# One head's queries and keys on the even partitions, the other's on the odd ones

## The chip, the cores and the metric

The kernel runs on one core of a Trainium2 chip. The metric is the device time of one execution in microseconds (us). Three executions of the kernel before took 274.06, 274.38 and 275.83 us; the median is 274.38. The profile is of another execution.

## The reference

Two stages. First, attention within chunks of 64 positions: 8 batches, 8 heads, 576 positions (9 chunks) and 64 features a head.

```
scores = q_c @ k_c^T / sqrt(64)          # per batch, head and chunk: 64x64
attn   = softmax(scores)                 # with 1e-9 added to the sum
out    = attn @ v_c                      # 64x64
```

The heads of a position are put side by side, which gives x of 4608 tokens by 512. Then a mixture of 8 experts: a token goes to the expert with the largest logit of x @ w_gate; each expert keeps the 80 tokens (the capacity) with the largest gate weight, and its rows of the output are gate * (relu(x @ w1[e]) @ w2[e]) (512 to 1024 to 512 features). All other rows of the output are zero. Everything is float32.

## The kernel before, in words

**Tiling of attention.** The positions are regrouped into 36 tiles of 128 rows (two chunks), taken two at a time in 18 pairs n = 0 to 17. One tile has four pairs of heads; the two heads of a pair lie on the 128 partitions, 64 features each.

**The buffers of queries and keys.** There are six (`qbufs`, L320), each 128 partitions by three blocks of 512 columns. On the lower 64 partitions (head 0) block 0 holds keys and block 1 queries; on the upper 64 (head 1) block 1 holds queries and block 2 keys. The rest, block 0 above and block 2 below, is set to zero once (L649, L650) and stays zero. So one matmul with block 1 as stationary operand and blocks 0 and 2 as moving operand (L344) gives the scores of both heads side by side: the contraction runs over all 128 partitions, and the zeros keep the heads apart. `load_qk` (L323) fills a buffer with two DMAs, one for each head: 64 rows of 4 KB (keys and queries side by side), 256 KB each. In DRAM the rows of a head lie next to each other.

**The buffers of values.** Six (`vbufs`, L330), filled by `load_v` (L333) with two DMAs of 64 rows of 2080 bytes each: head 0's rows go to the even partitions and head 1's to the odd ones, each to columns of its own. The score difference is written in the same interleaved order (L358), so the transposed probabilities match.

**One pair n in the loop (L697).** TensorE's order is written out by hand: `scores(n)` (L337), the transpose of x for the gate of pair n-3, `values` of pair n-2 (L380), the transpose of the probabilities of pair n-1 (L373), and on some pairs matmuls of the gate and of a threshold count. VectorE takes the row maxima and subtracts them (`maxima`, `minus`), divides by the sums (`divide`, L409), and does steps of the gate. ScalarE does the exponentials and the copies out of PSUM. SyncE issues the DMAs in program order: in iteration n the qk loads of pair n+3, the value loads of pair n+1 and, for tiles that are not kept on chip, a store of x to a scratch tensor `xs` in DRAM. Each buffer is overwritten three pairs later, and a load waits until its last reader is done. The framework works out these waits from the parts of buffers that instructions touch, and also makes a DMA wait for an earlier one of the same group of semaphores to land, so only some of them are under way at a time.

**Before and behind the loop.** The memsets of buffers and the first loads come first (L647 to L681): buffer 0 is set to zero by VectorE and loaded by SyncE, buffer 1 by GpSimd and ScalarE, the others by VectorE and SyncE. 25 matmuls without a use run meanwhile. From pair 15 on, SyncE also stores the tiles of x that were kept (1 MB each, L735) and loads the weights of the first two experts (`early_weights`, L631). Then comes a gating stage that finds each expert's tokens by a threshold, gathers of tokens by GpSimd from `xs` (L179), and the expert stage (L173 on), whose matmuls fill TensorE while SyncE loads weights of 2 MB and writes zero rows of the output.

Of the kernel before, what the change touches and what calls it, by code (L numbers as in the profile page):

```python
# [17 lines left out]
P = 128  # L18
# [39 lines left out]
def attention_moe(ctx: ExitStack, tc: tile.TileContext, qk, vv, wg, w1, w2, cap, cst, out):  # L58
# [225 lines left out]
    with ExitStack() as actx:  # L284
# [38 lines left out]
        def load_qk(i, eng=nc.sync):  # L323

            d = QKV["qk", i] = qbufs[i % (2 * NB)]
            for h in range(2):
                eng.dma_start(d[64 * h:64 * h + 64, 512 * h:512 * h + 1024],
                              qk[i // 2, i % 2, 64 * h:64 * h + 64])

        vbufs = [wk.tile([P, 2, VW], F32, name=f"vb{j}", tag=f"vb{j}", bufs=1)  # L330
# [313 lines left out]
        with tc.manual_schedule():  # L644
            warm = gk.tile([P, 2 * P], BF16, name="warm", tag="lv", bufs=LV)
            nc.vector.memset(warm, 0.0)
            for j, qb in enumerate(qbufs):  # L647
                eng = nc.gpsimd if j == 1 else nc.vector
                eng.memset(qb[64:P, 0:512], 0.0)  # L649
                eng.memset(qb[0:64, 1024:1536], 0.0)  # L650
                if j < 2:
                    load_qk(j, (nc.sync, nc.scalar)[j])
            nc.scalar.dma_start(ident, cst[:, C_ID:C_ID + P])
# [15 lines left out]
            for i in (2, 3):  # L669
                load_qk(i)  # L670
            for i in (0, 1):
                load_v(i)
            for i in (4, 5):
                load_qk(i)
# [407 lines left out]
```

## Time and profile before

| | |
|---|---|
| median of three runs | 274.38 us (274.06 to 275.83) |
| profiled execution | 277.03 us, of which its span 275.2 us |
| busy: TensorE matmul | 232.4 us (84%) |
| busy: VectorE / ScalarE / GpSimd | 119.0 / 66.5 / 57.0 us |
| DMA | 84.73 MB, mean 308 GB/s |
| qk loads | 70 on SyncE, 256 KB, 6.7 us from issue to landing (median); two more on ScalarE |
| value loads | 72 on SyncE, 130 KB, 6.6 us |
| weights of the experts | 12 loads of 2 MB and 8 of 1 MB |
| chain that ended last | `qb<-in_qk` 24%, first expert layer 16%, second 15% |

How to read it: the engines run beside each other, so their busy times don't add up to the span. The chain that ended last follows the last instruction back to what released it, step by step; its shares say what set the end. "Landing" is the time from a DMA's issue on a queue to its last byte. The profiled execution is 2.65 us longer than the median of the timed ones.

### The profile page before, as it was taken

The page shows a single profiled execution, that of the slowest core. Times are in us where ns is not written, and L with a number is a line of the kernel's source. Part 1 is how long each engine was busy: PE and PEld are TensorE (multiplying, and loading weights), DVE is VectorE, ACT ScalarE, POOL GpSimd, SP SyncE. Part 2 cuts the span into 40 slices and gives each one's busy share as a digit, 9 for nine tenths or more (in the row PEclk, how much of TensorE's full clock was granted, in tenths as well). Part 3 has the DMA queues.
Part 4 walks back from the last instruction along what each step waited for, and adds up shares of the span by engine and source line. Part 5 has one row for each costly group of instructions (what it writes and reads, how often), then busy time and mean ns, then how long its engine had stood idle before and what let it go on. Part 6 is the DMA issues. An engine that isn't in the chain of part 4 may idle for free.

```text
span 275.2 us, 7328 instructions
## 1 busy us (share of the span) xinstructions
PE 232.4 (84%) x3117; PEld 149.7 (54%) x3117; DVE 119.0 (43%) x263; ACT 66.5 (24%) x115; POOL 57.0 (21%) x167
## 2 busy tenths in 40 slices
PE   6773989979788977978868885899999999999990
PEld 4763778968667866766756574234333433333320
DVE  6545366876574846665735846011111211212110
ACT  1012123453251625352614410112020201101000
POOL 8003000121122222222373845300000000000081
PEclk9599799999999999999979779599999999999996
DMA  7998999999999999999999999999999999999431
GB/s 157 237 255 220 233 239 238 274 257 260 232 239 284 288 230 215 276 271 272 365 394 402 409 411 415 393 396 393 409 413 405 407 415 409 416 395 409 182 133 69
DMA packets 35718, 84.73 MB, mean 308 GB/s; under 512 B 4000, under 2 KB 4128, under 8 KB 35680
## 3 DMA queue, kind: packets, MB, share of 16 engines
q1 hardware_dynamic: 34416, 80.73, 93.0%
q0 software_dynamic: 960, 2.88, 2.7%
q10 hardware_dynamic: 304, 0.59, 1.0%
q8 instruction: 27, 0.44, 0.7%
q14 instruction: 11, 0.09, 0.1%
HBM read 64.00 MB, written 20.45 MB: 307 GB/s over the span
## 4 chain that ended last, share of the span: by engine, by line
PE 51%; DMA 39%; SPq 3%; POOL 3%; issue 2%; POOLq 0%; DVE 0%
DMA qb<-in_qk 24%; PE hc L204 16%; PE yc L237 15%; DMA vb<-in_vv 5%; PE o L403 5%; PE s L344 5%; DMA xs<-kept 4%; DMA w<-in_w 4%; DMA xgc<-xs,gic 2%; PE hpc L222 2%; SPq L335 2%; PE pt L369 2%; PE px L369 1%; PE xpc L192 1%; PE small L455 1%
## 5 line engine op out<-in xcount | busy, mean ns | idle before, releaser
L344 PE MATMUL s<-qb 128*64 128x128 f32 x576 | 42.3, 298 | 21.7 <-DMA qb<-in_qk 20.0
L344 PEld LDWEIGHTS s<-qb 128*64 128x64 f32 x576 | 35.6, 150 | 27.0 <-issue 22.4
L204 PE MATMUL hc<-w,xtc 128*32 128x512 f32 x384 | 45.6, 618 | 0.0
L237 PE MATMUL yc<-w,htc 128*32 128x512 f32 x384 | 42.3, 592 | 0.0
L403 PE MATMUL o<-vb,pT 128*64 128x130 f32 x576 | 38.0, 283 | 3.3 <-DMA vb<-in_vv 2.6
L354 DVE TENSOR_REDUCE mx<-s 128x16 f32<-128x1024 f32 x18 | 22.0, 1225 | 36.8 <-PE s L344 36.7
L403 PEld LDWEIGHTS o<-vb,pT 128*64 128x64 f32 x576 | 33.1, 139 | 4.8 <-issue 3.7
L237 PEld LDWEIGHTS yc<-w,htc 128*32 128x32 f32 x384 | 12.4, 110 | 28.3 <-issue 28.3
L204 PEld LDWEIGHTS hc<-w,xtc 128*32 128x32 f32 x384 | 12.6, 113 | 27.3 <-issue 26.7
L446 ACT COPY xT<-px 128x1024 f32<-128x1024 f32 x17 | 17.2, 1013 | 42.3 <-PE px L369 42.3
L378 ACT ACTIVATE pT<-pt 128x1024 f32<-128x1024 f32 x18 | 18.4, 1023 | 32.1 <-PE pt L369 32.1
L256 POOL DMA_INDIRECT out<-ysc,to x6 | 6.0, 993 | 88.5 <-SPq L933 86.1
L359 DVE TENSOR_TENSOR sm<-s,mx 128x1024 f32<-128x1024 f32 x18 | 22.1, 1228 | 0.6
L209 ACT ACTIVATE hsc<-hc 128x512 f32<-128x512 f32 x6 | 3.6, 597 | 65.3 <-PE hc L204 65.3
L242 DVE TENSOR_SCALAR ysc<-yc,gatec 128x512 f32<-128x512 f32 x6 | 4.5, 751 | 33.5 <-PE yc L237 33.5
L418 DVE TENSOR_TENSOR x<-o,rc 128x1024 f32<-128x1024 f32 (+1 forms) x14 | 15.0, 1072 | 0.5
L211 DVE TENSOR_SCALAR hsc<-hc 128x512 f32<-128x512 f32 x6 | 4.1, 691 | 25.2 <-PE hc L204 25.2
L520 POOL TENSOR_SCALAR u<-sx 128x4 f32<-128x4 f32 x8 | 1.6, 195 | 62.1 <-DVE sx L519 38.9
L369 PE MATMUL pt<-ct,sm 64*128 64x64 f32 x288 | 12.8, 229 | 1.2 <-ACT pT L378 1.2
L226 DVE COPY htc<-hpc 128x512 f32<-128x512 f32 x6 | 4.2, 692 | 22.0 <-PE hpc L222 22.0
L369 PEld LDWEIGHTS pt<-ct,sm 64*128 64x128 f32 x288 | 10.3, 139 | 4.3 <-issue 3.0
L545 ACT ACTIVATE lv<-io_b,bo 128x256 bf16<-128x256 bf16 x29 | 12.5, 497 | 0.4 <-DVE bo L526 0.4
(136 smaller groups left out, 233.8 us busy)
## 6 DMA issues: line engine op xcount, KB each, us to landing
w<-in_w SPq DMA_DIRECT2D x12, 2048.0 KB, 18.8
qb<-in_qk SPq DMA_DIRECT2D x70, 256.0 KB, 6.7
vb<-in_vv SPq DMA_DIRECT2D x72, 130.0 KB, 6.6
out<-zero SPq DMA_DIRECT2D x9, 1024.0 KB, 16.3
w<-in_w SPq DMA_DIRECT2D x8, 1024.0 KB, 12.6
xs<-x SPq DMA_DIRECT2D x10, 512.0 KB, 6.5
xs<-kept SPq DMA_DIRECT2D x3, 1024.0 KB, 8.8
xs<-x SPq DMA_DIRECT2D x4, 256.0 KB, 10.7
```

The source lines that it names most:

```text
L204: nc.tensor.matmul(h[o:o + 32, :], lhsT=xT[r][:, b, o:o + 32], rhs=getw(groups[r][g])[0][:, b, 512 * f:512 * f + 512], start=(b == 0), sto ...
L237: nc.tensor.matmul(y[o:o + 32, :], lhsT=hT[r][c // 4][:, c % 4, o:o + 32], rhs=getw(groups[r][g])[1][:, c, :], start=(c == 0), stop=(c == ...
L256: i = nc.gpsimd.indirect_dma_start(out=out, out_offset=bass.IndirectOffsetOnAxis(ap=to, axis=0), in_=ys, in_offset=None, bounds_check=NT * ...
L344: nc.tensor.matmul(ps[64 * u:64 * u + 64, t, P * pr:P * pr + P].rearrange("p (h k) -> p h k", h=2), lhsT=t8[:, 1, pr, u, :], rhs=t8[:, 0:3 ...
L354: nc.vector.tensor_reduce(d['mx'], d['s8'], axis=AX.X, op=ALU.max)
L359: nc.vector.tensor_tensor(d['sm'].rearrange("p c k h -> p h c k"), d['s8'], d['mx'][:, :, :, None].to_broadcast([P, 2, 8, 64]), op=ALU.sub ...
L369: nc.tensor.transpose(pm[:, u, 64 * c:64 * c + 64], src(c)[rows], ident[rows, rows])
L378: nc.scalar.activation(d['pT'], pt, AF.Exp, scale=0.125)
L403: nc.tensor.matmul(po[64 * u:64 * u + 64, o:o + 130].rearrange("p (h x) -> p h x", h=2), lhsT=d['pT'][:, u, c:c + 64], rhs=v[:, :, pr, u, ...
L418: nc.vector.tensor_tensor(TT[T][:, r:r + nt, :].rearrange("p r (k h e) -> p (r k) h e", k=4, h=2), pov[..., 0:64], rc[:, :, :, None].to_br ...
L446: nc.scalar.copy(dst, pm)
L545: nc.scalar.activation(lv, io_b, AF.Sign, bias=bo[:, rt:rt + 1], scale=-1.0)
```

## The change

`load_qk` writes head h to the partitions h, h+2, ..., that is to the even ones (h = 0) or the odd ones (h = 1). Columns, row size, source and queue are as before. As the zero parts are now every second partition of a block, the two memsets cover all 128 partitions of blocks 0 and 2, and the loads overwrite half of each. The score matmuls are the same; they sum over the partitions in another order.

```diff
             d = QKV["qk", i] = qbufs[i % (2 * NB)]
             for h in range(2):
-                eng.dma_start(d[64 * h:64 * h + 64, 512 * h:512 * h + 1024],
+                eng.dma_start(d[h:P:2, 512 * h:512 * h + 1024],
                               qk[i // 2, i % 2, 64 * h:64 * h + 64])
...
             for j, qb in enumerate(qbufs):
                 eng = nc.gpsimd if j == 1 else nc.vector
-                eng.memset(qb[64:P, 0:512], 0.0)
-                eng.memset(qb[0:64, 1024:1536], 0.0)
+                eng.memset(qb[:, 0:512], 0.0)
+                eng.memset(qb[:, 1024:1536], 0.0)
                 if j < 2:
                     load_qk(j, (nc.sync, nc.scalar)[j])
```

## Rows read from the trace of the kernel before

**Rows 1.** The page's 40 slices of the span: DMA busy tenths, and GB/s.

```profile
DMA  7998999999999999999999999999999999999431
GB/s 157 237 255 220 233 239 238 274 257 260 232 239 284 288 230 215 276 271 272 365 394 402 409 411 415 393 396 393 409 413 405 407 415 409 416 395 409 182 133 69
```

**Rows 2.** Busy time by stage: stretch, length, five engines, PEclk, DMA share, GB/s.

```profile
34.92:130.31 95.39, 81.77 (x1554) 70.42 (x1551) 61.66 (x113) 38.02 (x60) 17.19 (x76) 1.00 1.04 255
...
141.24:173.80 32.56, 25.31 (x305) 20.21 (x305) 18.19 (x84) 7.29 (x20) 17.95 (x43) 0.81 1.04 410
173.80:268.40 94.60, 94.23 (x836) 32.27 (x836) 12.59 (x20) 10.16 (x18) 7.15 (x12) 0.98 0.95 369
```

**Rows 3.** The chain in order of time: start us, us, what.

```profile
62.91 7.26 DMA qb<-in_qk
...
128.17 1.19 SPq L335
```

**Rows 4.** Waits of all engines: total us, times, longest us.

```profile
PE s L344 <- DMA qb<-in_qk: 20.0, 12, 4.7
```

**Rows 5.** Waits of SyncE's queue: total us, times, longest us.

```profile
SPq L327 <- DMA qb<-in_qk: 18.1, 31, 1.2
```

**Rows 6.** Timeline of SyncE: start us, us, line, operation, names, count.

```profile
8.47 2.41 SPq L335 DMA_DIRECT2D vb<-in_vv  x4
...
23.00 6.30 SPq L327 DMA_DIRECT2D qb<-in_qk  x10
...
126.06 3.30 SPq L335 DMA_DIRECT2D vb<-in_vv  x4
...
146.51 3.78 SPq L426 DMA_DIRECT2D xs<-x  x2
```

**Rows 7.** DMA issues near 23.0, 28.7, 126.1, 128.2, 146 to 152, 166 to 176: landing us.

```profile
qb<-in_qk SPq DMA_DIRECT2D x1, 256.0 KB, 3.5
...
qb<-in_qk SPq DMA_DIRECT2D x1, 256.0 KB, 7.9
...
vb<-in_vv SPq DMA_DIRECT2D x1, 130.0 KB, 5.8
...
vb<-in_vv SPq DMA_DIRECT2D x1, 130.0 KB, 4.6
...
xs<-x SPq DMA_DIRECT2D x4, 256.0 KB, 10.7
...
xgc<-xs,gic POOLq DMA_INDIRECT x6, 6.5
```

**Rows 8.** Timeline of TensorE, score and value matmuls: start us, us, [wait <- releaser].

```profile
34.92 1.97 PE L344 MATMUL s<-qb 128*64 128x128 f32 x32
...
42.12 1.97 PE L344 MATMUL s<-qb 128*64 128x128 f32 x32
...
59.20 1.09 PE L344 MATMUL s<-qb 128*64 128x128 f32 x16
...
131.14 1.99 PE L403 MATMUL o<-vb,pT 128*64 128x130 f32 x32
...
141.24 3.32 PE L403 MATMUL o<-vb,pT 128*64 128x130 f32 x32 [2.57 <-DMA vb<-in_vv]
```

**Rows 9.** Timeline of all engines from the start of the span.

```profile
0.73 4.06 SPq L327 DMA_DIRECT2D qb<-in_qk  x6
...
1.15 0.48 DVE L649 MEMSET qb<- 64x512 f32 x1 [0.16 <-issue]
1.29 0.52 POOL L650 MEMSET qb<- 64x512 f32 x1
...
1.78 0.48 DVE L650 MEMSET qb<- 64x512 f32 x1
...
7.52 0.93 DVE L655 MEMSET vb<- 128x1040 f32 x1 [0.17 <-issue]
...
30.07 1.70 PE L344 MATMUL s<-qb 128*64 128x128 f32 x16 [0.38 <-DMA qb<-in_qk]
```

## The prediction

> **What bounds the kernel now.** I read the slices of the page first. The DMA row stands at nine tenths or more from the second slice to the 37th (but for one at eight), yet the row of GB/s under it has two levels: 215 to 288 in slices 2 to 19, 365 to 416 in the next 18 [rows 1]. The 16 DMA engines count as busy in both; in the first they move far less. The table by stage puts numbers on it. From the fifth score block to the end of the last (34.92 to 130.31 us) the DMA share is 1.04 at 255 GB/s, while TensorE is busy 81.77 of 95.39 us; in the gating stage behind it the share is again 1.04, but at 410 GB/s; in the expert stage TensorE is busy 94.23 of 94.60 us [rows 2]. So attention is held by slow transfers and the experts by TensorE. The chain of waits says the same: it runs for long stretches through `qb<-in_qk`, in pieces such as one of 7.26 us [rows 3], and among TensorE's waits the score matmuls on that transfer lead with 20.0 us [rows 4]. SyncE too waited 18.1 us, 31 times, for an earlier qk load to land before it issued the next [rows 5]. All this is one queue that drains slowly.
>
> **How slow, and compared with what.** Ten qk loads of 256 KB are issued back to back, the first at 23.00 us, one every 0.63 us [rows 6]; the first lands 3.5 us after its issue, the tenth (issued 9 x 0.63 later, at 28.7) 7.9 us after [rows 7]. So they land (28.7 + 7.9 - 23.0 - 3.5) / 9 = **1.12 us apart**, 234 GB/s. The control is in the same kernel: a value load also moves 64 rows, but to every second partition. Four are issued from 126.06 us [rows 6]; the first lands 5.8 us after issue, the fourth, issued at 128.17 [rows 3], 4.6 after [rows 7]: (128.2 + 4.6 - 126.1 - 5.8) / 3 = 0.30 us for 130 KB, with some 0.03 of rounding, which scales to 0.53 to 0.65 us for 256 KB. The 410 GB/s of the gating stage [rows 2], where weights go to all 128 partitions, gives 256 KB / 410 = **0.64 us**. I take 0.64. What separates the qk loads from both is the 64 neighbouring partitions.
>
> [...]
>
> **The change, part by part.**
>
> *The loads.* Count, bytes and queue stay: 72 loads of 256 KB, each with 64 rows. Each goes from 1.12 to 0.64 us. Per pair that is 4 x 0.64 + 4 x 0.30 for the value loads, plus 1.3 for a 512 KB store at 410 GB/s where there is one: 5.1 us of DMA. SyncE needs 8 issues per pair, or 9 with a store, in ten of the 18 pairs: at 0.63 us each, as the ten qk loads went out [rows 6], 5.0 or 5.7, on average 5.4 us. TensorE's pace where no wait shows is (59.20 - 42.12) / 3 = 5.69 us a pair [rows 8]. So TensorE becomes the bound, with SyncE close behind.
>
> (a) *From the fifth score block to the last*, now 95.39 us. If only TensorE's idle time goes, it saves 95.39 - 81.77 = 13.6 us [rows 2]. At the pace of 5.69, 13 blocks and the last one's 1.97 take 75.9 us, and 19.5 are saved [rows 8]. The three blocks of the pace lack the threshold tallies that every second pair has from the ninth on, and busy time holds them, so I take a value nearer the first: **15.5**, ends 13.6 and 19.5.
>
> (b) *The start.* The fourth score block's second half runs at 30.07 us, after a wait for its load [rows 9]. In the code that load's second half is the 23rd issue on SyncE from the value load at 8.47 us on [rows 6]. At 0.63 us each it goes out at 8.47 + 22 x 0.63 = 22.3, and lands 3.5 - (1.12 - 0.64) = 3.0 us later, at 25.3: 4.8 us earlier, of which I take **4.5** for waits that stay. SyncE's waits for earlier landings are what goes here; the issue rate is late next. Ends: 3, if most of these waits stay, and 6, if the small loads among the 22 issue faster.
>
> (c) *The tail of attention.* The last two value blocks wait 2.57 us for `vb`, then take 3.32 us, where two others took 1.99 [rows 8]. Their loads sit in the queue behind stores and weights that SyncE issued late. With SyncE no longer behind, both go: 2.57 + 1.33 = 3.9. Ends 0 and 3.9; **3**, as the stores of the kept tiles and the first experts' weights still crowd that queue.
>
> (d) *The gather.* The first gather of tokens takes 6.5 us beside a backlog of weights [rows 7]; with the backlog gone earlier it might take the 3.5 of a load into a short queue [rows 7]. Ends 0 and 3; **1**. The expert stage itself moves as a block, covered by TensorE's 94.23 busy us. Were weights late there, TensorE would wait; it does not now, and their loads will meet a shorter queue.
>
> *The memsets.* They keep their 512 columns and double their partitions. A 64x512 one takes 0.48 us on VectorE, a 128x1040 one 0.93 [rows 9], so partitions are free: 0.
>
> *A wait added at the start.* The memsets now touch partitions that the first loads write. SyncE's first load waits for VectorE's memset of columns 0:512 (end 1.63 us in place of its issue at 0.73), the second for that of 1024:1536 (2.26 us) [rows 9]; four more qk loads are queued behind, all before the value load that is held until 8.47 us anyway. ScalarE's two loads wait for GpSimd's memsets, the second of which ends at 1.81 us [rows 9]; the load of the identity is behind them. About 0.9 us late, against four loads that drain 4 x 0.48 = 1.9 us faster: 0, already inside (b). If the loads stayed slow, up to 1 us would show.
>
> **Sum:** 15.5 + 4.5 + 3 + 1 = 24. The profiled execution took 277.03 us (span 275.2), 2.65 above the median of 274.38; none of the terms is known to be in that difference, so I take the sum off the median: 274.4 - 24 = **250.4** (and 253 for a run like the profiled one).
>
> **The rivals.**
>
> *Another engine binds first.* SyncE has 5.4 of 5.69 us filled, and its instructions wait in order for TensorE's release of buffers. If these waits add 0.9 us a pair, the pace is 6.5, the stretch 13 x 6.5 + 2 = 86.5, and (a) falls to 8.9; with (b) and nothing for (c) and (d), 274.4 - 13.4 = 261. Against it: loads run three pairs ahead, so a lag of one pair costs nothing. Chance 0.08.
>
> *Nothing changes.* [...] Chance 0.05.
>
> *Slower.* The two halves of a buffer now interleave by partitions and share columns 512:1024. If the planner that places waits treats them as one block, the second half's load waits for the first to land: 3.0 - 0.64 = 2.4 us, twice a pair. SyncE's pace becomes 5.4 + 4.8 = 10.2 us, the stretch 13 x 10.2 + 2 = 135, 39 more than now: about 313. It decides above some 0.85 us of wait per half, where 5.4 + 1.7 reaches today's (95.39 - 1.97) / 13 = 7.2 us a pair. Against it: the last stores of `x` write interleaved blocks of rows of one tensor, and the second went out within 3.78 us of the first [rows 6], though such stores take 10.7 us to land [rows 7]. Chance 0.07.
>
> *The forecast* keeps 0.80; its own range is 274.4 - 33 = 241 to 274.4 - 16.6 = 258, by the ends of the terms. All upper ends together are unlikely, so the range starts at 243; it reaches to 262 to take in the busy SyncE. About 1% (2.7 us) is what a measurement of this kernel can tell from no change. Faster by more: 0.80 + 0.08 = 0.88; same: 0.05; slower: 0.07.
>
> **What would show it.** In the profile after: `qb` loads that land about 0.64 us apart, GB/s near 300 in attention at a DMA share clearly under 1, the score matmuls' wait on `qb` down from 20 us to a few, score blocks 5.7 to 6.0 us apart, the fourth block's second half near 25.5, no 2.57 us at the last value blocks. Blocks 6.5 apart with TensorE idle would mean SyncE or VectorE; landings still 1.12 apart, that partitions are not the cause; a gap of some 3 us between the two halves' issues, the planner's wait. The forecast is wrong if the experts then wait for weights and give the gain back.

## The result, and the profile after

The change made the kernel **5.5% faster**: medians of 259.81 us after and 274.69 us before (four runs each), ratio 0.9446, 95% interval 0.9403 to 0.949. The forecast was 250.4 with a range of 243 to 262: the direction and the range held, the gain was 14.9 us where 24 had been forecast. The profiled execution after took 258.25 us (span 256.5), 1.6 below its median, while that of before lay 2.3 above its own; of the 18.7 us between the two spans some 3.9 are therefore differences between executions, not the change.

The slices of the page after, DMA busy tenths and GB/s, against [rows 1]:

```profile
DMA  5888988998998799999999999999999999999241
GB/s 197 277 254 270 366 299 281 312 337 281 299 293 290 249 289 312 329 319 347 397 406 411 412 417 389 397 393 411 418 408 402 416 408 411 410 397 404 107 162 38
```

The attention part moves about 250 to 370 GB/s in place of 215 to 288, and the DMA engines are no longer full there. The table by stage of the kernel after, in the columns of [rows 2] (attention from the fifth score block to the end of the last, the stretch from there to the first gather, the experts):

```profile
33.53:111.96 78.43, 78.43 (x1554) 69.78 (x1551) 61.40 (x113) 37.48 (x60) 16.71 (x75) 1.00 0.91 297
111.96:146.76 34.80, 28.09 (x400) 22.64 (x400) 21.15 (x75) 12.60 (x28) 18.47 (x55) 0.85 1.04 391
154.45:248.66 94.21, 94.21 (x836) 31.78 (x836) 12.30 (x19) 10.16 (x18) 6.96 (x11) 0.98 0.96 372
```

In the first stretch TensorE is busy for all of its 78.43 us: it is the bound now. A DMA share of 1.04 is reached only in the stretch behind it. What the transfers do, first SyncE's timeline after (against the ten loads of [rows 6]):

```profile
20.03 6.29 SPq L327 DMA_DIRECT2D qb<-in_qk  x10
```

and the landing times of its first, fourth, ninth and tenth load (issued near 20.0, 21.9, 25.1 and 25.7 us, as in [rows 7]):

```profile
qb<-in_qk SPq DMA_DIRECT2D x1, 256.0 KB, 3.1
...
qb<-in_qk SPq DMA_DIRECT2D x1, 256.0 KB, 4.5
...
qb<-in_qk SPq DMA_DIRECT2D x1, 256.0 KB, 4.5
...
qb<-in_qk SPq DMA_DIRECT2D x1, 256.0 KB, 5.7
```

The fourth and the ninth wait equally long, so from one to the other loads land as far apart as they are issued: (25.1 - 21.9) / 5 = 0.64 us, with some 0.02 of rounding. From the first to the tenth, as the 1.12 us of before were worked out, it is (25.7 + 5.7 - 20.0 - 3.1) / 9 = 0.92 us, because two landings in between came over a microsecond late: the third load took 4.3 us where the second took 3.1, and the tenth took 5.7. Now TensorE's timeline after, with the columns of [rows 8]:

```profile
23.89 1.09 PE L344 MATMUL s<-qb 128*64 128x128 f32 x16 [2.20 <-DMA qb<-in_qk]
...
26.48 1.98 PE L344 MATMUL s<-qb 128*64 128x128 f32 x16 [1.50 <-DMA qb<-in_qk]
...
29.43 3.51 PE L403 MATMUL o<-vb,pT 128*64 128x130 f32 x32
33.53 1.97 PE L344 MATMUL s<-qb 128*64 128x128 f32 x32
...
110.00 1.97 PE L344 MATMUL s<-qb 128*64 128x128 f32 x32
...
121.51 2.00 PE L403 MATMUL o<-vb,pT 128*64 128x130 f32 x32 [0.96 <-DMA vb<-in_vv]
```

The pace of the score blocks is (110.00 - 33.53) / 13 = 5.88 us. The waits of the kernel after (total us, times, longest), against [rows 4]:

```profile
PE s L344 <- DMA qb<-in_qk: 7.6, 5, 2.8
...
POOL w L639 <- DMA xs<-kept: 2.5, 1, 2.5
...
PE o L403 <- DMA vb<-in_vv: 1.0, 1, 1.0
```

The wait for qk loads fell from 20.0 to 7.6 us, all of it at the start. And the chain of waits after, in the tail (start us, us, what):

```profile
121.19 11.78 DMA xs<-kept
...
133.08 0.31 POOL w L639 x2
...
146.76 6.44 DMA xgc<-xs,gic
```

A store of a kept tile needs 11.78 us to land, GpSimd waits for it with a copy into a weight buffer (L639, which holds back the second expert's weights), and what GpSimd does next stands on the way to the gather.

### The profile page after: what moved, and what is told of

The parts are those of the page before. It is cut to its first block, busy times and chain, and to the rows that moved or that the text cites. A ratio compares the mean times of both kernels' runs of the same rounds, so it can differ in the third digit from the quotient of the medians.

```text
span 256.5 us, 7329 instructions
## 1 busy us (share of the span) xinstructions
PE 229.5 (89%) x3117; PEld 148.0 (58%) x3117; DVE 118.5 (46%) x263; ACT 66.1 (26%) x115; POOL 56.8 (22%) x167
## 4 chain that ended last, share of the span: by engine, by line
PE 76%; DMA 11%; DVE 3%; POOL 3%; issue 2%; SPq 1%; ACT 1%; POOLq 0%; ACTq 0%
PE hc L204 17%; PE yc L237 16%; PE o L403 13%; PE s L344 12%; DMA xs<-kept 5%; PE pt L369 4%; PE px L369 4%; DMA qb<-in_qk 4%; PE small L455 3%; DMA xgc<-xs,gic 3%; PE hpc L222 2%; PE xpc L192 1%; DVE qb L650 1%; DVE qb L649 1%; SPq L335 1%
## 5 line engine op out<-in xcount | busy, mean ns | idle before, releaser
L344 PE MATMUL s<-qb 128*64 128x128 f32 x576 | 38.2, 287 | 7.7 <-DMA qb<-in_qk 7.6
L344 PEld LDWEIGHTS s<-qb 128*64 128x64 f32 x576 | 33.4, 144 | 10.8 <-issue 6.8
L237 PEld LDWEIGHTS yc<-w,htc 128*32 128x32 f32 x384 | 12.4, 110 | 28.3 <-issue 28.3
L211 DVE TENSOR_SCALAR hsc<-hc 128x512 f32<-128x512 f32 x6 | 4.2, 692 | 25.3 <-PE hc L204 25.3
## 6 DMA issues: line engine op xcount, KB each, us to landing
w<-in_w SPq DMA_DIRECT2D x8, 1024.0 KB, 12.4
```

Source lines behind the costliest of these rows:

```text
L237: nc.tensor.matmul(y[o:o + 32, :], lhsT=hT[r][c // 4][:, c % 4, o:o + 32], rhs=getw(groups[r][g])[1][:, c, :], start=(c == 0), stop=(c == ...
L344: nc.tensor.matmul(ps[64 * u:64 * u + 64, t, P * pr:P * pr + P].rearrange("p (h k) -> p h k", h=2), lhsT=t8[:, 1, pr, u, :], rhs=t8[:, 0:3 ...
```

## The experiments

For each, the stretch of 40 to 100 us gives one row (length, five engines, PEclk, DMA share, GB/s). GB/s divided by the DMA share is an estimate of what the engines would move if they were never idle: the pace of the transfers themselves, value loads and stores included. Kernel before: 256 / 1.05 = 244.

```profile
40.00:100.00 60.00, 52.37 (x1009) 45.34 (x1007) 38.83 (x73) 23.89 (x38) 10.91 (x48) 1.00 1.05 256
```

Kernel after: 294 / 0.91 = 323.

```profile
40.00:100.00 60.00, 60.00 (x1187) 53.45 (x1183) 46.30 (x88) 28.32 (x47) 13.38 (x60) 1.00 0.91 294
```

**E1, the wide memsets alone.** The kernel before with

```diff
-                eng.memset(qb[64:P, 0:512], 0.0)
-                eng.memset(qb[0:64, 1024:1536], 0.0)
+                eng.memset(qb[:, 0:512], 0.0)
+                eng.memset(qb[:, 1024:1536], 0.0)
```

> The wide memsets alone: qk loads go to the lower and upper 64 partitions as before. Theory (the partitions that a load reaches set its pace): landings stay about 1.12 us apart, the DMA share in attention stays near 1.04 at 255 GB/s, time within 1% of before (272 to 277.5; the first loads go out 0.9 us later). Rival (the memsets' new form, after which VectorE finishes a microsecond sooner and the value loads start earlier, gives part of the gain): 270 or less.

Measured: 275.41 us, ratio 1.003 (0.997 to 1.009). Its row:

```profile
40.00:100.00 60.00, 53.28 (x1008) 46.51 (x1006) 40.28 (x75) 24.57 (x39) 10.91 (x48) 0.97 1.04 261
```

261 / 1.04 = 251, near the 244 of before. The whole gain comes with the loads' partitions, and the late first loads cost nothing that can be measured.

**E2, half of the loads.** The kernel after, but only even buffers interleaved (memsets to match):

```diff
-                eng.dma_start(d[h:P:2, 512 * h:512 * h + 1024],
+                rows = slice(h, P, 2) if i % 2 == 0 else slice(64 * h, 64 * h + 64)
+                eng.dma_start(d[rows, 512 * h:512 * h + 1024],
```

> Only buffers 0, 2 and 4 are loaded to every second partition, the odd ones to 64 neighbouring partitions. Theory (transfers no longer bind once a pair's DMA time is below TensorE's 5.88 us): a pair needs 2 x 0.64 + 2 x 1.12 + 4 x 0.30 and 1.3 for a store in ten of 18 pairs, on average 5.4 us, so the pace of the score blocks stays near 5.9 and the time is 259 to 263. Rival (each load that is made faster gives its share): half of the gain, 266 to 269.

Measured: 263.91 us, ratio 0.9615 (0.929 to 0.994). Its row, and three score blocks of its TensorE timeline:

```profile
40.00:100.00 60.00, 58.08 (x1137) 51.24 (x1131) 45.40 (x84) 28.33 (x46) 12.62 (x56) 1.00 1.00 280
```

```profile
52.33 1.97 PE L345 MATMUL s<-qb 128*64 128x128 f32 x32
...
87.64 1.09 PE L345 MATMUL s<-qb 128*64 128x128 f32 x16
...
114.27 2.18 PE L345 MATMUL s<-qb 128*64 128x128 f32 x32
```

280 / 1.00 = 280 lies half way between 244 and 323, yet the six blocks from the first of these rows to the second take (87.64 - 52.33) / 6 = 5.89 us each, as in the kernel with all loads interleaved. From 87.64 on blocks wait for loads again, and the last four take (114.27 - 87.64) / 4 = 6.66 us each. So half of the change gives the whole pace for a while, which fits loads that were issued ahead being used up, and then the transfers bind again: the theory holds only for the first part, and its 5.4 us of DMA a pair were too few. The interval of the time is too wide to tell theory and rival apart by itself.

**E3, another order of the first loads.** The kernel after with

```diff
-            for i in (2, 3):
+            for i in (2, 3, 4, 5):
                 load_qk(i)
-            for i in (0, 1):
-                load_v(i)
-            for i in (4, 5):
-                load_qk(i)
-            for i in (2, 3):
+            for i in (0, 1, 2, 3):
                 load_v(i)
...
-            for i in range(4, NBV):
-                load_v(i)
...
                     if n < 2:
                         load_qk(2 * (n + NB) + 1)
+                    if n == 0:
+                        for i in range(4, NBV):
+                            load_v(i)
```

The last two value buffers are now loaded behind the qk loads of pair 3.

> The changed kernel with its first loads in another order: the qk loads of buffers 4 and 5 ahead of the first value loads, in the time in which SyncE waited for VectorE's memset of a value buffer, and the last two value buffers behind the qk loads of pair 3. Theory (the start is held by when SyncE can issue, and the waits cost twice since the clock falls after them): the fifth score block starts at 25 to 28 us in place of 33.5, and the total is 253 to 256. Rival (SyncE's 5.4 us of issuing per pair becomes the bound as soon as TensorE starts earlier): the last score block ends at 109 us or later in place of 112, total 257 to 260.

Measured: 257.8 us, ratio 0.9394 (0.919 to 0.960). Score blocks of its TensorE timeline, the fifth and the last's second half:

```profile
28.09 1.97 PE L344 MATMUL s<-qb 128*64 128x128 f32 x32
...
107.73 1.09 PE L344 MATMUL s<-qb 128*64 128x128 f32 x16 [0.48 <-DMA qb<-in_qk]
```

its waits:

```profile
POOL w L639 <- DMA xs<-kept: 3.3, 1, 3.3
PE o L403 <- DMA vb<-in_vv: 2.7, 1, 2.7
```

and its chain:

```profile
146.45 6.49 DMA xgc<-xs,gic
```

The fifth block starts 5.4 us earlier and the last ends 3.1 us earlier (108.8 against 112.0), but the gather goes out at 146.45 against 146.76: both waits in the tail grew, and the gain is gone before the gather. The rival's total (257 to 260) came out, but neither side had this reason. By its interval the time can't be told from that of the change (0.9446).

**E4, the kept stores early, on SyncE's queue.**

```diff
-DEFER = {15: [0], 16: [2], 17: [4]}
+DEFER = {6: [0], 10: [2], 11: [4]}
```

> The changed kernel, with the three stores of the kept tiles (1 MB each) issued in pairs 6, 10 and 11, which store nothing else, in place of 15, 16 and 17. Theory (the tail behind attention is held by the DMA queue: GpSimd waits 2.5 us for the last kept store and the last value blocks wait for their loads): both waits go, and the time falls by 2 to 4.5 us to 255 to 258. Rival (the tail is held by its chain of small steps, or attention has no DMA time to spare): within 1 us of the changed kernel, or above it.

Measured: 261.82 us, ratio 0.9541 (0.938 to 0.971). Its waits and its chain:

```profile
PE s L344 <- DMA qb<-in_qk: 12.4, 8, 4.4
```

```profile
149.67 6.42 DMA xgc<-xs,gic
```

The wait of GpSimd for the store went, and its last score block ends at 117.5, so the stretch to the gather is 32.2 us in place of 34.8: the theory's half on the tail holds. But attention lost 5.5 us: the score matmuls' wait for qk loads rose from 7.6 to 12.4 us, which fits each 1 MB store standing ahead of qk loads in the one queue. The sum is as the rival had it; by its interval the time can't be told from that of the change.

**E5, 64 neighbouring partitions from 32 to 95.** The kernel after with

```diff
-            for h in range(2):
-                eng.dma_start(d[h:P:2, 512 * h:512 * h + 1024],
-                              qk[i // 2, i % 2, 64 * h:64 * h + 64])
+            src = qk[i // 2, i % 2]
+            eng.dma_start(d[32:96, 0:1024], src[0:64])
+            eng.dma_start(d[0:32, 512:1536], src[64:96])
+            nc.scalar.dma_start(d[96:P, 512:1536], src[96:P])
```

> Head 0 goes in one load to the 64 neighbouring partitions 32 to 95, head 1 in two loads of 32 rows to partitions 0 to 31 (SyncE) and 96 to 127 (ScalarE's queue); no load uses every second partition. Theory (what counts is that a load covers parts of both the lower and the upper 64 partitions): head 0's loads are as fast as interleaved ones, about 0.64 us per 256 KB, GB/s in attention near 297, time 258 to 264. Rival (what counts is that the rows of a load are not neighbours): 256 KB stay near 1.1 us, GB/s near 255, 270 to 276.

Measured: 289.07 us (four executions from 284.02 to 289.38), where the kernel before, measured beside it, took 275.56. Its row, and SyncE's waits:

```profile
40.00:100.00 60.00, 49.94 (x906) 43.51 (x902) 36.57 (x66) 21.52 (x33) 8.17 (x37) 0.94 0.73 216
```

```profile
SPq L336 <- DMA qb<-in_qk: 19.0, 13, 4.7
```

The time is far from both expectations, and for a reason that neither had: SyncE's value loads (L336) waited 19.0 us, 13 times, for qk loads to land. Its chain points to those on ScalarE's queue: a qk load goes out straight behind a score block at 58.40 us, with no issue of SyncE between, lands 3.10 us later, and a value load follows at 61.52. The transfers themselves have a pace of 216 / 0.73 = 296, well above the 244 of loads to the lower or upper half, though none of this kernel's qk loads goes to every second partition. Single loads say it more directly. Four on SyncE's queue, issued at 27.04, 28.19, 28.74 and 29.42 us, go in turn to partitions 0 to 31 (128 KB) and 32 to 95 (256 KB); their landing times:

```profile
qb<-in_qk SPq DMA_DIRECT2D x1, 128.0 KB, 5.3
...
qb<-in_qk SPq DMA_DIRECT2D x1, 256.0 KB, 4.8
...
qb<-in_qk SPq DMA_DIRECT2D x1, 128.0 KB, 5.0
...
qb<-in_qk SPq DMA_DIRECT2D x1, 256.0 KB, 5.0
```

So they land at 32.3, 33.0, 33.7 and 34.4 us. The 256 KB across the middle come some 0.65 us behind the load ahead of them, as interleaved ones do; the 128 KB in one half take as long for half the bytes. So the pace doesn't need rows that aren't neighbours: these 64 rows, with 32 in each half, have it.

**E6, opposite halves on two queues.** The kernel before, with loads of odd buffers on ScalarE's queue, upper half first:

```diff
-            for h in range(2):
+            if i >= 2 and i % 2:
+                eng = nc.scalar
+            for h in ((1, 0) if i % 2 else (0, 1)):
```

> The layout of before, but loads of odd buffers go out on ScalarE's queue, upper half first, so that transfers to the lower and to the upper 64 partitions are more often under way together. Theory (each half of the partitions takes data at a limited pace of its own): GB/s in attention rises from 255 to 275 or more and the time falls to 262 to 271. Rival (one transfer to 64 neighbouring partitions is slow whatever runs beside it): 272 or more, GB/s near 255.

Measured: 279.17 us, ratio 1.012 (1.005 to 1.019). Its row, and a wait of ScalarE:

```profile
40.00:100.00 60.00, 54.90 (x1034) 48.72 (x1032) 42.58 (x74) 23.99 (x37) 9.48 (x42) 0.96 0.98 246
```

```profile
ACT pT L380 <- DMA qb<-in_qk: 30.3, 7, 14.2
```

246 / 0.98 = 251: no faster than the 244 and 251 of before and E1, so the theory's gain did not come. But ScalarE stood still for 30.3 us behind its loads, and the trace doesn't show how often opposite halves were under way together; whether two such transfers could share the engines better stays open.

**E7 and E8, the kept stores early on ScalarE's queue**, alone and with the order of E3:

```diff
-DEFER = {15: [0], 16: [2], 17: [4]}
+DEFER = {6: [0], 10: [2], 12: [4]}
...
             for n in range(NPAIR):
                 odd = n % 2
+                for T in DEFER.get(n, ()):
+                    store(2 * T, 4, nc.scalar)
...
-                for T in DEFER.get(n, ()):
-                    store(2 * T, 4)
```

> The changed kernel with the three kept stores issued early (before pairs 6, 10 and 12) on ScalarE's queue. Theory (in the run with early stores on SyncE's queue, attention lost 5 us since each store stood in line ahead of the qk loads and SyncE had no slack; the tail itself gained 2.6 us): the tail from the last score block to the first gather is again near 32 us, the score matmuls' wait on qb stays near the changed kernel's 7.6 us and the time is 256 to 258. Rival (the 3 MB cost attention their transfer time on any queue): 259.5 or more.

> The early kept stores on ScalarE's queue together with the new order of the first loads. Theory (start and tail are held one behind the other by the DMA queue: an earlier start alone was given back in the tail, since 46 MB have to pass before the gather): both gains stay, the last score block ends at 107 to 110 us, the first gather goes out near 141, time 252 to 255. Rival (the queue as a whole binds; the gain of one eats that of the other): 256 or more.

Measured: E7 271.86 us, ratio 0.9889 (0.982 to 0.996); E8 266.94, 0.9611 (0.953 to 0.969). Both theories fell; both times lie where the rivals had them, though the waits show another reason than theirs. SyncE's waits in E7:

```profile
SPq L327 <- DMA xs<-kept: 12.3, 2, 10.0
```

SyncE's qk loads waited up to 10.0 us for a store on another engine's queue to land, though they share no buffer with it. In that longest wait the store itself took only 4.35 us, from its issue at 45.71; for the other 5.65 us SyncE stood waiting for ScalarE to issue it. That the framework counts the DMAs of both queues in the same groups of semaphores is the author's reading of these waits, which no run shows directly. A second queue is no way round the first here, which fits the long waits in E5 and E6.

**E9, GpSimd's copies left out**, so that SyncE's weight loads wait for the kept store themselves:

```diff
-                early_weights(k, bo[:, 28 + 4 * (k - 6):29 + 4 * (k - 6)])
+                early_weights(k)
```

> The changed kernel without GpSimd's copies into the weight buffer of the second expert (L639), so that GpSimd no longer waits for the last kept store; SyncE's loads wait for it themselves. Theory (that wait of 2.5 us lies on the path to the gather, behind which GpSimd still has the parts of the last keys to make): the stretch from the last score block's end to the first gather falls from 34.8 to 32 to 33.5 us, the time to 257 to 259 (ratio to before 0.935 to 0.942). Rival (the stretch has another end as late, the queue or the small steps): ratio 0.943 or more.

Measured: 258.79 us, ratio 0.9419 (0.935 to 0.949). Its wait in the tail, and its chain:

```profile
PE o L403 <- DMA vb<-in_vv: 3.3, 1, 3.3
```

```profile
114.13 7.70 DMA vb<-in_vv
...
132.59 10.20 DMA xs<-x
...
146.81 7.14 DMA xgc<-xs,gic
```

GpSimd's wait is gone, the last score block ended at 110.3, and still the gather goes out at 146.81: another way to it, through the last value loads and the last store of x, is just as long. The stretch became 36.5 us, against the theory. The time lies in the theory's range all the same, but by its interval it can't be told from that of the change.

**E10, E11 and E12, another order in the tail**, alone, with the order of E3, and with that and E9:

```diff
-DEFER = {15: [0], 16: [2], 17: [4]}
+DEFER = {15: [0], 16: [2, 4]}
...
-EARLY = {15: [0], 16: [1], 17: [2, 3], 18: [4], 19: [5]}
+EARLY = {17: [0, 1, 2, 3], 18: [4], 19: [5]}
```

> The changed kernel with another order of the same transfers in the tail: the kept stores go out in pairs 15, 16 and 16, all weights of the first expert behind them from pair 17 on. Theory (the tail waits for the last kept store and the last value loads, which stand in one queue behind weights that are needed 30 us later): both waits (2.5 and 1.0 us) go, no byte moves elsewhere, ratio to before 0.932 to 0.940. Rival (what binds is the sum of bytes before the experts, 46 MB before the gather, in any order): the expert stage or the gather then waits for weights, ratio 0.943 or more.

> The new order of the first loads and the new order of the tail together. Theory (with the tail no longer held by the queue's order, the 3 us that an earlier start gives at the last score block come through): last score block ends at 107 to 110 us, the stretch to the gather is 32 to 34 us, ratio to before 0.918 to 0.930. Rival (the sum of bytes binds): the stretch grows again by what the start gained, ratio 0.934 or more.

> As the run with both orders, and without GpSimd's copies. Theory: with the kept stores early GpSimd has no wait left to lose, so it is within 0.5% of the run with both orders. Rival (the copies also hold back weights that disturb the gather, so leaving them out is a loss): slower by 1% or more.

Measured: E10 258.89 us, ratio 0.9383 (0.930 to 0.946); **E11 255.5**, 0.931 (0.925 to 0.937); E12 255.56, 0.9297 (0.923 to 0.936). The chain of E11, and its waits:

```profile
143.30 6.48 DMA xgc<-xs,gic
```

```profile
PEld hc L204 <- DMA w<-in_w: 2.1, 1, 2.1
...
PE hc L204 <- DMA w<-in_w: 1.2, 1, 1.2
```

In E10 the gather goes out at 145.3 and in E11 at 143.3 us: with the weights behind the stores the order of the queue no longer gives the whole start back. It gives half of it back: the last score block ends at 107.9 in E11 and 111.8 in E10, so the stretch to the gather is 35.5 us in place of 33.6, against E11's theory of 32 to 34. And the first expert layer now waits for its weights (2.1 and 1.2 us in E11, 2.0 and 1.1 in E10), a wait that the kernel after doesn't have. So both sides were partly right: the order held the tail, and behind it the bytes that have to pass before the experts begin. E12 shows nothing left in GpSimd's copies. E11 beats both kernels: its interval ends below that of the change (0.9403).

## Why the prediction was right, and where its sizes were off

**The mechanism was right.** Loads of 64 rows land 0.64 us apart where nothing delays them (taken: 0.64), and 0.92 with the two late landings, in place of 1.12; the value loads were a good control, E1 leaves the gain to the partitions alone, and E5 leaves out the interleaving as such. *Nothing changes* fell with this, and *slower* too: both halves of a buffer are issued 0.63 us apart, so no wait was put between them.

**(a) Attention: right.** 95.39 [rows 2] became 78.43 us, 17.0 saved where 15.5 were taken (ends 13.6 and 19.5). TensorE became the bound, as its 78.43 busy us of 78.43 show. *Another engine binds first* did not happen: the pace is 5.88 us. One execution of the old transfers is not like the next, though: in E1's profile the same stretch took 91.88 us (36.99 to 128.87), which would make the gain 13.45.

**(b) The start: too large.** The fourth block's second half came at 26.48 in place of 30.07 us [rows 9], a gain of 3.6; 25.3 to 25.6 had been worked out. Its load went out near 21.9, about as forecast (22.3), but took 4.5 us to land, not 3.0. And the fifth block came only 1.4 us earlier, 33.53 against 34.92 [rows 8], outside the ends of 3 and 6. What was missing is the clock, shown by the stages of the kernel after and, below it, of the kernel before:

```profile
25.80:32.60 6.80, 6.12 (x62) 5.70 (x64) 2.45 (x2) 1.01 (x1) 0.00 (x0) 0.50 0.99 362
```

```profile
28.00:31.30 3.30, 2.92 (x28) 2.55 (x27) 0.00 (x0) 0.00 (x0) 0.00 (x0) 0.50 1.06 235
```

From 25.8 to 32.6 us, in and behind the waits of 2.2 and 1.5 us for qk loads, the granted clock is 0.50, and 32 value matmuls took 3.51 us where others took 2.00. Before, the clock was that low only from 28.0 to 31.3 us, behind a wait of 4.70 us for a qk load that ended at 27.81. The working ended at a load's landing and took the matmuls behind it at their old length. How much the start gains is uncertain, too: with the same first loads and the same transfers as the kernel after, the fifth block came at 32.12 in E4, 31.53 in E9 and 33.35 in E10, and with the old transfers at 36.99 in E1. Over these profiles the gain lies between 1.4 and 5.5 us.

**(c) The tail: no gain shown.** 3 were taken of 3.9. The stretch from the last block's end to the gather went from 35.75 (130.31 to 166.06) to 34.80 us: 0.95. In E1, with the old transfers and the same tail, it is 34.28 (128.87 to 163.15), so not even this is clear of the differences between executions. The wait for value loads fell from 2.57 [rows 8] to 0.96, but GpSimd's wait for the last kept store grew to 2.5 us, from 0.61 in the kernel before:

```profile
152.31 0.39 POOL L639 COPY w<-bo 128x1 f32<-128x1 f32 x2 [0.61 <-DMA xs<-kept]
```

And the wait that (c) priced wasn't on the chain of the kernel before. In the tail that chain ran through a weight load and the last kept store:

```profile
130.56 9.89 DMA w<-in_w
...
140.92 11.27 DMA xs<-kept
```

The step said that the weights and stores "still crowd that queue" and then priced only one of the waits behind it. E3 and E9 show the point: the last score block ended at 112.0, 108.8 and 110.3 us in the kernel after, E3 and E9, and the gather went out at 146.76, 146.45 and 146.81. Over these 3 us it hangs on the queue, not on when attention ends.

**(d) The gather: nothing.** 6.44 us against 6.49; the DMA share there is 1.03, against 1.04 before, so no shorter queue was met.

**The sum.** Between the profiles 17.0 + 1.4 + 0.95, less 0.6 that the part from the gather on took more (109.1 to 109.7 us), make 18.7 us. The rest to the measured 14.9 is the difference between executions named above. With E1's profile (span 273.5) in place of that of before, the same parts are 13.45 + 3.46 - 0.52 + 0.61 = 17.0 us: attention gave most of it, but each part is known to some 2 to 4 us only. The forecast's 24 added terms as if each came through by itself; (b) and (c) share one queue, and what (b) brings, (c) can take back, as E3 shows.

**The range held partly by luck.** By the ends of the terms it was 241 to 258 us, and the measured 259.8 lies outside. It had been stretched to 262 for a busy SyncE, which did not come. Two sums of the working are off as well, without weight for the result: the upper ends add up to 32.4 and not 33, which makes 242, and 0.9 us on SyncE's 5.4 make a pace of 6.3 and not 6.5.

## What to carry to other kernels

When DMA engines count as busy but move less than elsewhere in the same kernel, compare transfers by GB/s over DMA share and look at which partitions they touch; here 64 rows of 4 KB spread over both halves of the partitions landed 0.64 us apart where nothing delayed them, and 64 in one half 1.12. Before adding gains along a chain, ask which later point is set by a queue that must deliver a given lot by then: gains ahead of it come through only as far as that queue runs ahead too (in E3, 3.1 us at the last score block were 0.3 at the gather). Price what stands behind a wait at the clock granted there (here 0.50 from 25.8 to 32.6 us). And look at a second profile of the same transfers before you explain 2 us of one stage.

## What had not been expected

DMAs on another engine's queue held up the first queue's loads (E7: 12.3 us, E5: part of 19.0 us), so that moving 3 MB of stores to ScalarE's queue, and earlier, cost 12 us (271.86 against 259.81). The wide memsets let VectorE start its memsets 0.54 us apart in place of 0.64; the idle of 0.16 us before every second one [rows 9] is gone. And now and then a landing comes late by itself, as those of the third and the tenth of the ten loads above; no run here shows why.
